# The w_v phase's pools open during the last w_k product; its data come as quarter tiles

## The chip, the cores and the metric

The kernel runs on one core of one Trainium2 chip. The metric is the device time of one execution in microseconds (us), and the median of several runs is what is compared. The engines are PE (TensorE, matrix products), DVE (VectorE), ACT (ScalarE), POOL (GpSimd) and SP (SyncE, which here only issues transfers). ACT also issues some transfers. Each engine carries out its own instructions in the order in which they stand in its queue, and an instruction that has to wait holds back all that stand behind it.

## The reference, cut to what matters

```python
# attention: batch 8, heads 8, sequence 576, head size 64
kv = einsum('bhsd,bhse->bhde', k, v); out = einsum('bhsd,bhde->bhse', q, kv)
x  = out / sqrt(mean(out**2) + 1e-6) * g_norm           # then (8, 576, 512)
# first mixture: d_model 512, d_ff 1024
k  = maximum((mu_k*x + (1-mu_k)*x_prev) @ w_k, 0)
r  = 1 / (1 + exp(-((mu_r*x + (1-mu_r)*x_prev) @ w_r)))
x  = r * ((k*k) @ w_v)
# second mixture: 4 experts, head size 64: top-2 gates, causal softmax attention in each expert
q, k, v = x @ wq[e], x @ wk[e], x @ wv[e]
out += gate[e] * (softmax(mask(q @ k.T / 8)) @ v @ wo[e])
```

The change concerns the middle part: the end of `@ w_k`, all of `@ w_v`, and the start of the second mixture.

## The kernel before

Every fp32 matrix is split into a high and a low part (`split`, L59: ACT writes the high part, L60, then DVE subtracts to get the low part, L61), and each product is three matmuls (`mm3`, L63 to L67): high·high, high·low, low·high.

The work runs through three phases. `phase_a` (L172) does attention and then, for each batch 0 to 7, the groups of w_r (`r_group`, 8 of them) and of w_k (`k_group`, 16 of them, 12 matmuls each). A `k_group` ends in ACT's `rl` (relu, L444), POOL's `ksq` (the square, L446) and a store to DRAM, `kkd`; an `r_group` ends in a store `sgd`. `phase_v` (L605) loads them back, per batch, as `kin` (two halves of the sequence, 1152 KB each, `load`, L126) and `sgv` (1152 KB, `load_s`, L132), multiplies by w_v and stores the result as `x2d`. `phase2` is the second mixture, which reads `x2d`.

The product with w_v is Strassen's scheme with seven products of quarter matrices. The left operands a11, a12, s1, s2, s4, a22, s3 were made from w_v long before and stay in SBUF. The right operands of a batch are made by `prep(b)` (L137): the quarters b11, b21, b12, b22 of `kin` and the differences t1 to t4 (`tv`, L149, on DVE for t1, t2 and on POOL for t3, t4), each split into a `kk` tile by ACT (L60) and DVE (L61). The `kk` tiles rotate through 5 buffers. `products(b)` issues seven products of 24 matmuls each (`prod`, L616 to L622), two output halves m = 0, 1 of 12 matmuls; results lie in PSUM banks `acc`, of which there are 8. Product 1 (a11·b11) stays in its bank `qa` and is added to by product 4 (s2·t2) and product 7 (s3·t3); product 3 (s1·t1) stays in `qd` and is added to by product 5 (s4·b22). ACT copies what has to be kept (`vp`, `vq`, `vu`, L626); DVE adds the parts (`ct`, L631), POOL multiplies by the gate in `sgv` (L633).

In the course of `phase_v` the weights of the second mixture are loaded too (`weights2`, L69 to L112): `wst` tiles in 2 buffers (4 of w_qk, 4 of w_vg, 2 of w_o; load L88), scaled on DVE for w_qk (L90), and split by ACT and DVE (`wqh`, `wgh`, `woh` on ACT; `wql`, `wgl`, `wol` on DVE). So are the first rows of the second mixture: `x20i` (L690) from `x2d` of batch 0, split into `x20h` on ACT (L698). A scheduler that works from a modelled timeline chooses the order on every engine; the order in the program gives only what depends on what. So `weights2`, which the program starts at batch 1, and `x20i`, which it names at batch 7, stand much earlier in the queues than in the program.

PSUM and SBUF are handed out by pools. The pool of `phase_v`, `sbv`, and its 8 banks opened after `phase_a` had closed its own; only the first batch's `kin` (pool `k0`, opened at L601 in batch 6) and three operands of it (`first_prep`, run at n = 12, 15, 18 of batch 7's groups, L588) were made earlier. `phase2` starts on ACT with loads `x2in` (L721, one buffer), their split `x2h` (L727; the low part `x2l` on POOL, L728), the copies `qs`, `ks` of the q and k products, and the exponentials `pr` (L854).

## Time and profile before

| | |
|---|---|
| median of 3 runs | 1027.13 us (1027.01 to 1028.32) |
| the profiled execution | 1032.2 us, of which the span from the first to the last instruction is 1030.3 us |
| PE busy | 974.2 us, 95% of the span |
| DVE, ACT, POOL busy | 646.0, 540.8, 417.5 us |
| mean granted clock of TensorE | 0.974 of full speed |
| w_v products on PE | 450.0 to 640.4 us of the span |

A row of a timeline gives the start, the duration, the engine, the line and the operation, and in brackets how long the engine had sat idle and what it had waited for. Matmuls overlap by their pipeline, so the count of matmuls in a stretch says more of PE than its busy time. Lines are those of the kernel before; in the kernel after they are shifted by 1 to 8.

### The profile page before, as it was taken

How to read it: one execution, taken by the hardware profiler on the slowest of the kernel's cores; microseconds unless marked ns; L12 is line 12 of the kernel's file. 1: busy time of each engine (PE TensorE's matmuls, PEld its weight loads, DVE VectorE, ACT ScalarE, POOL GpSimd, SP SyncE). 2: the span in 40 equal slices, each digit the busy share in tenths (PEclk: the TensorE clock that was granted, in tenths of full speed). 3: DMA queues.
4: the chain of work that ended last, by engine and by line, in shares of the span. 5: the costliest groups of instructions: out<-in, count | busy, mean ns of one | idle time of the engine just before them, and what ended most of it. 6: DMA issues, size and time to landing. Idle time of an engine off the chain costs nothing.

```text
span 1030.3 us, 21148 instructions
## 1 busy us (share of the span) xinstructions
PE 974.2 (95%) x7960; PEld 886.0 (86%) x7960; DVE 646.0 (63%) x1538; ACT 540.8 (52%) x1334; POOL 417.5 (41%) x510
## 2 busy tenths in 40 slices
PE   5679899999999999999899999799999999999998
PEld 3359879999999999999799999788989898888886
DVE  4868976455362638239999995366565655656552
ACT  4656755555565556444454443255553635464544
POOL 0005544131222314267777786255251615344321
PEclk9889988999999999999989999899999999999999
DMA  9463362635536225257756631200110202020102
GB/s 349 153 193 125 130 209 81 207 108 181 166 124 206 89 76 167 99 193 251 247 202 213 229 139 47 93 22 27 67 59 36 81 13 93 3 92 26 48 13 81
DMA packets 80180, 127.20 MB, mean 123 GB/s; under 512 B 7120, under 2 KB 57808, under 8 KB 78032
## 3 DMA queue, kind: packets, MB, share of 16 engines
q1 hardware_dynamic: 60592, 97.68, 28.0%
q10 hardware_dynamic: 19488, 28.19, 8.4%
q8 instruction: 63, 1.03, 0.4%
q14 instruction: 37, 0.30, 0.1%
HBM read 78.66 MB, written 47.19 MB: 122 GB/s over the span
## 4 chain that ended last, share of the span: by engine, by line
PE 67%; DMA 12%; DVE 7%; ACT 5%; POOL 5%; issue 2%; SPq 0%; ACTq 0%; DVEq 0%; POOLq 0%
PE acc L65 15%; PE acc L66 14%; PE acc L67 14%; PE acc L621 12%; DMA x2in<-x2d 3%; PE acc L918 3%; PE pt L891 3%; PE s L842 2%; DMA vraw<-in_w_v 2%; ACT pr L854 2%; POOL x2l L728 2%; POOL pr L871 2%; DMA kin<-kkd 2%; PE po L313 1%; DMA kt<-in_k 1%
## 5 line engine op out<-in xcount | busy, mean ns | idle before, releaser
L446 POOL TENSOR_TENSOR ksq<-rl 128x288 f32<-128x288 f32 x128 | 96.5, 756 | 173.8 <-ACT rl L444 141.8
L66 PE MATMUL acc<-mixl,wkh 128*128 128x288 f32 x512 | 154.3, 301 | 0.0
L65 PE MATMUL acc<-mixh,wkh 128*128 128x288 f32 x512 | 152.7, 298 | 0.0
L67 PE MATMUL acc<-mixh,wkl 128*128 128x288 f32 x512 | 151.7, 296 | 0.0
L854 ACT ACTIVATE pr<-pr,nm 128x256 f32<-128x256 f32 (+4 forms) x144 | 83.2, 580 | 75.0 <-DVE nm L808 74.0
L871 POOL TENSOR_SCALAR pr<-pr,rc,wg 128x512 f32<-128x512 f32 (+3 forms) x128 | 76.7, 615 | 104.7 <-DVE wg L801 46.2
L621 PE MATMUL acc<-kk,wh_s 128*128 128x288 f32 x512 | 104.7, 299 | 7.1 <-ACT vq L626 4.9
L409 DVE TENSOR_TENSOR mixl<-xm,mixh 128x288 fp32r<-128x288 f32 x120 | 57.2, 512 | 86.3 <-ACT mixh L417 86.3
L633 POOL TENSOR_TENSOR sgv<-ct,sgv 128x288 f32<-128x288 f32 x64 | 93.3, 1483 | 36.5 <-DVE ct L631 34.9
L66 PEld LDWEIGHTS acc<-mixl,wkh 128*128 128x128 f32 x512 | 97.2, 190 | 1.6
L444 ACT ACTIVATE rl<-acc 128x288 f32<-128x288 f32 x128 | 51.7, 406 | 87.8 <-PE acc L67 80.3
L67 PEld LDWEIGHTS acc<-mixh,wkl 128*128 128x128 f32 x512 | 97.6, 191 | 0.0
L65 PEld LDWEIGHTS acc<-mixh,wkh 128*128 128x128 f32 x512 | 97.1, 190 | 0.1
L621 PEld LDWEIGHTS acc<-kk,wh_s 128*128 128x128 f32 x512 | 83.1, 190 | 8.2 <-ACT vq L626 5.5
L65 PE MATMUL acc<-mixh,wrh 128*128 128x288 f32 x256 | 79.5, 311 | 0.5 <-ACT rl L444 0.5
L621 PE MATMUL acc<-kk,wh_a 128*128 128x288 f32 x384 | 78.5, 299 | 0.0
L808 DVE CUSTOM_DVE_ANT_0 pr<-s,mask 128x256 f32<-128x256 f32 (+4 forms) x144 | 66.9, 481 | 17.0 <-PE pt L891 13.2
L67 PE MATMUL acc<-mixh,wrl 128*128 128x288 f32 x256 | 76.8, 300 | 0.0
L66 PE MATMUL acc<-mixl,wrh 128*128 128x288 f32 x256 | 76.5, 299 | 0.2 <-ACT mixl L407 0.2
L621 PE MATMUL acc<-kk,wl_s 128*128 128x288 f32 x256 | 76.0, 297 | 0.0
L65 PE MATMUL acc<-x2h,wqh 128*128 128x320 f32 (+1 forms) x240 | 74.4, 310 | 0.0
L66 PE MATMUL acc<-x2l,wqh 128*128 128x320 f32 (+1 forms) x240 | 71.0, 296 | 0.0
(201 smaller groups left out, 2687.4 us busy)
## 6 DMA issues: line engine op xcount, KB each, us to landing
kkd<-ksq SPq DMA_DIRECT2D x128, 144.0 KB, 1.7
kin<-kkd SPq DMA_DIRECT2D x16, 1152.0 KB, 6.3
qt<-in_qT SPq DMA_DIRECT2D x32, 288.0 KB, 4.7
sgd<-sg ACTq DMA_DIRECT2D x64, 144.0 KB, 3.0
sgv<-sgd SPq DMA_DIRECT2D x8, 1152.0 KB, 5.2
x2d<-sgv SPq DMA_DIRECT2D x8, 1152.0 KB, 4.6
out<-ob SPq DMA_DIRECT2D x28, 288.0 KB, 2.1
kt<-in_k SPq DMA_DIRECT2D x24, 256.0 KB, 4.9
```

What stands on the lines that cost most here:

```text
L65: nc.tensor.matmul(ps, wh(i), xh(i), start=(i == 0), stop=False)
L66: nc.tensor.matmul(ps, wh(i), xl(i), start=False, stop=False)
L67: nc.tensor.matmul(ps, wl(i), xh(i), start=False, stop=(i == n - 1))
L409: nc.vector.tensor_sub(xl[:, p, :], xp, xh[:, p, :].bitcast(F32))
L444: nc.scalar.activation(rl, acc[:, :HS], AF.Relu)
L446: nc.gpsimd.tensor_mul(sq, rl, rl)
L621: nc.tensor.matmul(q[:, :HS], a[:, i, ms_], c[:, i, :], start=(start and i == 0 and n == 0), stop=(stop and i == KH - 1 and n == 2), skip_ ...
L633: nc.gpsimd.tensor_mul(g, c, g)
L808: nc.vector.tensor_tensor_reduce(out=pr[:R, k0:k0 + kn], in0=s[:R, :kn], in1=mk, scale=1.0, scalar=lo, op0=ALU.add, op1=ALU.min, accum_out ...
L854: nc.scalar.activation(pr[:, :L], pr[:, :L], AF.Exp, bias=nm, scale=-1.0, accum_out=sms[b, p, j][:, e2:e2 + 1])
L871: nc.gpsimd.tensor_scalar(pr[:, :L], pr[:, :L], rc[:, r:r + 1], wg, op0=ALU.mult, op1=ALU.mult)
L891: nc.tensor.transpose(pt[:, (i - i0) * P:(i - i0 + 1) * P], pr[:, k1 - P:k1], ident)
```

## The change

- The pool of `phase_v` (`sbv`) and its PSUM pool (`psv`) open in the middle of batch 7, at its first `k_group` (n = 8), after the pools of the attention front and of w_r (`psf`, `fr`, `w1`) have been closed. To make that possible the pools change sides in SBUF (`vb`, `fr`, `w1`, `sbv` right; `wk`, `w2`, `x2p` left) and the tiles `mix`, `rl`, `ksq` move to the `wk` pool.
- PSUM is split. Four banks `acc` of `phase_a` are kept through `phase_v`. The four banks of the front (`po`) become two banks `qa` and two banks `qd`, which serve only products 1, 4, 7 and products 3, 5. Before, all of these took turns in 8 banks.
- `load(0)` is issued there, and `first_prep` is `prep(0)`, run one step behind each `k_group` from n = 13 on, so that all seven operands of batch 0 are in the program before the last `k_group`.
- `kin` comes as four quarter tiles of 576 KB (5 buffers) in place of two halves (3 buffers), `sgv` as two halves of 576 KB (3 buffers) in place of one tile (2 buffers). `x2d` is stored in two halves, the first after product 5, the second at the end of the batch.
- `weights2` starts at batch 2 in the program, not at batch 1.

```diff
@@ load, load_s
-                kin[b, h] = pools[-1].tile([P, KF, HS], F32, name="kin", bufs=3 if b else 2)
-                nc.sync.dma_start(kin[b, h], kkd[b][:, :, h * HS:(h + 1) * HS])
+                for i in range(2):
+                    kin[b, i, h] = W["sv"].tile([P, KH, HS], F32, name="kin", bufs=5)
+                    nc.sync.dma_start(kin[b, i, h], kkd[b][:, KH * i:KH * i + KH, h * HS:(h + 1) * HS])
-            sgt[b] = pools[-1].tile([P, KD, S], F32, name="sgv", bufs=2)
-            nc.sync.dma_start(sgt[b], sgd[b])
+            for i in range(2):
+                sgt[b, i] = W["sv"].tile([P, KD // 2, S], F32, name="sgv", bufs=3)
+                nc.sync.dma_start(sgt[b, i], sgd[b][:, 2 * i:2 * i + 2, :])
@@ prep
-            hl = pools[-1].tile([P, 2, KH, HS], F32R, name="kk", bufs=5 if len(pools) > 1 else 3)
+            hl = W["sv"].tile([P, 2, KH, HS], F32R, name="kk", bufs=5)
@@ phase_a
-                    po = ps.tile([P, 2, 512], F32, name="po", bufs=2)
+                    po = pf.tile([P, 2, 512], F32, name="po", bufs=2)
+                first_prep = iter(())
                 for n, (g, h, m) in enumerate(groups):
+                    if not nxt and n == 2 * KD:
+                        for _ in mk:
+                            pass
+                        stf.close()
+                        W["st"] = ExitStack()
+                        W["sv"] = W["st"].enter_context(tc.tile_pool(name="sbv", bufs=1, side="right", reuse_waits="tile"))
+                        W["psv"] = W["st"].enter_context(tc.tile_pool(name="psv", bufs=1, space=PSUM, reuse_waits="tile"))
+                        load(0)
+                        first_prep = prep(0)
                     g(b, h, m)
-                    if not nxt and n in (12, 15, 18):
+                    if n > 2 * KD + 3:
                         run(first_prep)
@@ phase_v
-                def bank():
-                    return ps.tile([P, 512], F32, name="acc", bufs=8)
+                def bank(name="acc"):
+                    if name == "acc":
+                        return W["acc"].tile([P, 512], F32, name="acc", bufs=4)
+                    return W["psv"].tile([P, 512], F32, name=name, bufs=2)
-                    qa[m] = bank()
+                    qa[m] = bank("qa")
-                    qd[m] = bank()
+                    qd[m] = bank("qd")
+                nc.sync.dma_start(x2d[b][:, :2, :], sgt[b, 0])
...
-                nc.sync.dma_start(x2d[b], sg)
+                nc.sync.dma_start(x2d[b][:, 2:, :], sgt[b, 1])
-                if b == 1:
-                    W["k0"].close()
+                if b == 2:
                     w2 = weights2()
-                    if b > 0 and n in (1, 3, 5):
+                    if b > 1 and n in (1, 3, 5):
                         run(w2)
```

What the scheduler makes of it on the engines: up to the last groups of batch 7 the orders are the same. Then three places differ that matter here.

PE, at the end of `phase_a`. Before, the last of batch 7's `k_group`s (`mixh`, `mixl` by `wkh`, `wkl`) is followed by product 1 of batch 0:

```order
L65 MATMUL acc<-mixh,wkh 128x288
L66 MATMUL acc<-mixl,wkh 128x288
L67 MATMUL acc<-mixh,wkl 128x288
L621 MATMUL acc<-kk,wh_a_93 128x288 x2
L621 MATMUL acc<-kk,wl_a_94 128x288
L621 MATMUL acc<-kk,wh_a_93 128x288 x2
```

After, four of the 16 `k_group`s are left when product 1 begins; here is the one between the two parts of it and the change to product 3 (`qd`):

```order
L65 MATMUL acc<-mixh,wkh 128x288
L66 MATMUL acc<-mixl,wkh 128x288
L67 MATMUL acc<-mixh,wkl 128x288
L629 MATMUL qa<-kk,wh_a_93 128x288 x2
L629 MATMUL qa<-kk,wl_a_94 128x288
L629 MATMUL qa<-kk,wh_a_93 128x288 x2
L629 MATMUL qa<-kk,wl_a_94 128x288
L629 MATMUL qa<-kk,wh_a_93 128x288 x2
L629 MATMUL qa<-kk,wl_a_94 128x288
L629 MATMUL qd<-kk,wh_s_97 128x288 x2
L629 MATMUL qd<-kk,wl_s_98 128x288
```

So 30 matmuls of w_v have moved ahead of the last 36 of w_k, and from batch 1 on product 2, whose banks are `acc`, now begins before product 1, whose banks are `qa`: per batch 20 matmuls of product 2, 12 of product 1 (m = 0), 4 of product 2, 8 of product 3 (`qd`), then 12 of product 1 (m = 1).

ACT, where it splits the weights of the second mixture between the copies and operands of w_v. Before, in batches 1 and 2 (`vp`, `vq`, `vu` are the kept copies; `kk` the operands):

```order
L60 ACTIVATE wqh<-wst 128x512
L626 ACTIVATE vu<-acc 128x288
L60 ACTIVATE wqh<-wst 128x512
L60 ACTIVATE kk<-kin 128x1152
L626 ACTIVATE vu<-acc 128x288
L60 ACTIVATE wgh<-wst 128x260
L60 ACTIVATE kk<-tv 128x1152 x2
L60 ACTIVATE wgh<-wst 128x260
L626 ACTIVATE vu<-acc 128x288
L698 ACTIVATE x20h<-x20i 128x256 x4
L60 ACTIVATE kk<-kin 128x1152
L626 ACTIVATE vu<-acc 128x288
```

After, in batch 1, `vq` to the last `vu`:

```order
L634 ACTIVATE vq<-qd 128x288
L60 ACTIVATE kk<-kin 128x1152
L634 ACTIVATE vq<-qd 128x288
L60 ACTIVATE wgh<-wst 128x260
L634 ACTIVATE vu<-qa 128x288
L60 ACTIVATE woh<-wst 128x512
L60 ACTIVATE kk<-kin 128x1152
L634 ACTIVATE vu<-qa 128x288
L703 ACTIVATE x20h<-x20i 128x256 x4
L60 ACTIVATE kk<-tv 128x1152 x2
L60 ACTIVATE woh<-wst 128x512
L634 ACTIVATE vu<-qa 128x288
```

The first `wqh` has moved from behind batch 0's last `vu` to behind its first `vu`, and the last `woh` from behind batch 2's second `vq` to ahead of batch 1's last `vu`. The order of the kinds among themselves is the old one: `wqh`, `wgh`, then `woh` and `x20h` between operands.

ACT, at the start of the second mixture, before:

```order
L727 ACTIVATE x2h_8054<-x_7806 128x320 x4
L60 ACTIVATE qs<-acc 128x256
L60 ACTIVATE ks<-acc 128x256
L721 DMA x2in<-x2d_58 128x4x256
L727 ACTIVATE x2h_8296<-x2in 128x256 x4
L721 DMA x2in<-x2d_58 128x4x320
L854 ACT_TABLE_LOAD
L854 ACTIVATE pr,sm<-pr,nm 128x128 x2
L854 ACTIVATE pr,sm<-pr,nm 128x256 x2
L60 ACTIVATE qs<-acc 128x320
L60 ACTIVATE ks<-acc 128x320
```

and after:

```order
L734 ACTIVATE x2h_8110<-x_7860 128x320 x4
L60 ACTIVATE qs<-acc 128x256
L60 ACTIVATE ks<-acc 128x256
L728 DMA x2in<-x2d_58 128x4x256
L734 ACTIVATE x2h_8352<-x2in 128x256 x4
L728 DMA x2in<-x2d_58 128x4x320
L60 ACTIVATE qs<-acc 128x320
L861 ACT_TABLE_LOAD
L861 ACTIVATE pr,sm<-pr,nm 128x128 x2
L861 ACTIVATE pr,sm<-pr,nm 128x256 x2
L60 ACTIVATE ks<-acc 128x320
```

The copy `qs` of 320 columns has moved ahead of the table load and of the four exponentials; `ks` has stayed behind them.

On SP, the loads of batch 1's `kin` and the first half of its `sgv` stand among the last `kkd` stores, where they stood behind them; the `wst` loads stand behind the last `kkd` store in both. The load of `x20i` stands behind the first `wst` of w_o, and before it stood behind the second `wst` of w_vg.

## Rows read from the trace of the kernel before

**Rows 1.** The page, part 1: busy us (share of the span) xinstructions of each engine.
```profile
PE 974.2 (95%) x7960; PEld 886.0 (86%) x7960; DVE 646.0 (63%) x1538; ACT 540.8 (52%) x1334; POOL 417.5 (41%) x510
```

**Rows 2.** Windows of 10 us: per engine busy (xinstructions), then PEclk, DMA share, GB/s.
```profile
480.00:490.00 10.00, 10.00 (x77) 10.00 (x76) 10.00 (x11) 2.93 (x4) 7.74 (x6) 1.00 0.95 333
490.00:500.00 10.00, 9.48 (x71) 9.24 (x70) 9.72 (x12) 5.45 (x8) 3.46 (x4) 1.00 0.59 211
500.00:510.00 10.00, 8.30 (x63) 8.07 (x62) 8.46 (x8) 5.37 (x12) 10.00 (x7) 1.00 0.73 231
510.00:520.00 10.00, 5.10 (x25) 4.52 (x25) 9.68 (x10) 5.93 (x10) 8.46 (x6) 0.67 0.80 287
520.00:530.00 10.00, 10.00 (x65) 10.00 (x64) 8.69 (x8) 4.20 (x5) 5.38 (x4) 0.82 0.34 121
```

**Rows 3.** Waits in 485 to 530: who waited for what, us, times, longest.
```profile
PE acc L621 <- ACT vq L626: 4.9, 2, 3.1
PE acc L621 <- DVE ct L631: 1.7, 1, 1.7
ACT wgh L60 <- DMA wst<-in_w_vg: 7.9, 3, 3.3
ACT wqh L60 <- DVE wst L90: 7.2, 2, 6.7
ACT woh L60 <- DMA wst<-in_w_o: 3.4, 1, 3.4
```

**Rows 4.** Timeline of ACT: start, us, line, operation [idle before <-releaser].
```profile
510.33 0.42 ACT L60 ACTIVATE wgh<-wst 128x260 fp32r<-128x260 f32 x1 [3.33 <-DMA wst<-in_w_vg]
```

**Rows 5.** Timeline of DVE around the first products.
```profile
450.18 1.36 DVE L149 TENSOR_TENSOR tv<-kin,tv 128x1152 f32<-128x1152 f32 x1 [28.46 <-PE acc L67]
458.29 3.47 DVE L61 TENSOR_TENSOR kk<-tv,kk 128x1152 fp32r<-128x1152 f32 x1
474.81 2.86 DVE L90 TENSOR_SCALAR wst<-wst 128x256 f32<-128x256 f32 x2
```

**Rows 6.** DMA issues in 445 to 512: xcount, KB each, us from issue to landing.
```profile
kin<-kkd SPq DMA_DIRECT2D x7, 1152.0 KB, 6.2
wst<-in_w_qk SPq DMA_DIRECT2D x4, 256.0 KB, 6.7
x20i<-x2d SPq DMA_DIRECT2D x1, 512.0 KB, 7.1
```

**Rows 7.** Windows: one steady batch of w_v products.
```profile
579.80:602.10 22.30, 22.30 (x170) 22.30 (x169) 20.86 (x18) 11.02 (x15) 18.02 (x11) 1.00 0.63 213
```

**Rows 8.** Timeline of DVE in the steady loop.
```profile
575.40 3.38 DVE L61 TENSOR_TENSOR kk<-kin,kk 128x1152 fp32r<-128x1152 f32 x1
578.71 0.45 DVE L631 TENSOR_TENSOR ct<-acc,vq 128x288 f32<-128x288 f32 x1
601.20 0.45 DVE L631 TENSOR_TENSOR ct<-acc,vq 128x288 f32<-128x288 f32 x1
```

**Rows 9.** Timeline of PE where product 1 of a steady batch begins.
```profile
573.14 0.43 PE L621 MATMUL acc<-kk,wh_a 128*128 128x288 f32 x2
```

**Rows 10.** Timeline of ACT at the start of the last phase.
```profile
655.41 1.28 ACT L854 ACT_TABLE_LOAD   x1 [2.55 <-POOL x2l L728]
658.47 0.41 ACT L60 ACTIVATE qs<-acc 128x320 fp32r<-128x320 f32 x1
```

**Rows 11.** Timeline of PE at the same place.
```profile
659.46 0.58 PE L65 MATMUL acc<-wgh,x2h 128*128 128x260 f32 x1 [5.71 <-DVE qs L61]
```

**Rows 12.** Windows: TensorE right behind that.
```profile
657.00:663.00 6.00, 3.54 (x16) 3.54 (x17) 1.94 (x7) 2.21 (x10) 0.58 (x2) 0.50 0.27 99
```

**Rows 13.** DMA issues in 640 to 645.
```profile
x2d<-sgv SPq DMA_DIRECT2D x1, 1152.0 KB, 5.2
x2in<-x2d ACTq DMA_DIRECT2D x1, 512.0 KB, 8.0
```

**Rows 14.** DMA issues in 655 to 760, the 512 KB loads.
```profile
x2in<-x2d ACTq DMA_DIRECT2D x2, 512.0 KB, 4.0
```

More of the change, by code (lines that the diff above doesn't have):

```diff
@@ L122, in tile_kernel @@
     blk = {}
-    kin, ops, sgt, pools = {}, {}, {}, []
+    kin, ops, sgt = {}, {}, {}
     def load(b):
@@ L147, in diff @@
         def diff(x, y, eng):
-            t = pools[-1].tile([P, KH, HS], F32, name="tv", bufs=2 if len(pools) > 1 else 1)
+            t = W["sv"].tile([P, KH, HS], F32, name="tv", bufs=2)
             eng.tensor_sub(t, x, y)
             return t
-        operand("b11", quarter(0, 0))
+        b11, b21, b12, b22 = [kin[b, i, h] for h in range(2) for i in range(2)]
+        operand("b11", b11)
         yield
-        operand("b21", quarter(1, 0))
-        t1 = diff(quarter(0, 1), quarter(0, 0), nc.vector)
+        operand("b21", b21)
+        t1 = diff(b12, b11, nc.vector)
         yield
@@ L157, in prep @@
         yield
-        t2 = diff(quarter(1, 1), t1, nc.vector)
+        t2 = diff(b22, t1, nc.vector)
         operand("t2", t2)
-        t4 = diff(t2, quarter(1, 0), nc.gpsimd)
+        t4 = diff(t2, b21, nc.gpsimd)
         yield
-        operand("b22", quarter(1, 1))
-        t3 = diff(quarter(1, 1), quarter(0, 1), nc.gpsimd)
+        operand("b22", b22)
+        t3 = diff(b22, b12, nc.gpsimd)
         yield
@@ L355, in scaled @@
                     for a in range(2):
-                        po = ps.tile([P, 2, 512], F32, name="po", bufs=2)
+                        po = pf.tile([P, 2, 512], F32, name="po", bufs=2)
                         for i in range(2):
@@ L399, in mix @@
                 xT = xTs[b]
-                xh, xl = mixed[b, h, which] = [sb.tile([P, KD, HS], F32R, name=f"mix{u}", bufs=3) for u in "hl"]
+                xh, xl = mixed[b, h, which] = [wk.tile([P, KD, HS], F32R, name=f"mix{u}", bufs=3) for u in "hl"]
                 def low(p):
@@ L667, in products @@
                     gated(1, m, 0, sub, u3, qc[m][:, :HS])
-                nc.sync.dma_start(x2d[b], sg)
+                nc.sync.dma_start(x2d[b][:, 2:, :], sgt[b, 1])
                 yield
-            pools.append(sb)
+            load_s(0)
             load(1)
-            load_s(0)
-            for _ in first_prep:
-                pass
             for b in range(B):
@@ L701, in phase_v @@
                     pass
+        W["st"].close()
+        W["ps"].close()
         W["vb"].close()
```

44 lines of the change are left out of this document (19 added, 25 removed).

## The prediction

> **What bounds the kernel now.** I read the page's busy times first: PE is busy 95% of the span [rows 1], so apart from places where PE stands still nothing but fewer matmuls could help, and the change takes none away. So the question is where PE stands still, or runs at half clock, near the code that is touched. The windows show one such place inside the w_v products [rows 2]: PE starts 77 matmuls in 480–490, as in any full window, then 71, 63, 25 and 65. That is (6 + 14 + 52 + 12) = 84 short. A batch of w_v is 7 × 24 = 168 matmuls, and the same `ct` stands at 578.71 and again at 601.20 one batch later [rows 8], so a matmul takes 22.49 / 168 = 0.134 us; 84 of them are **11.2 us lost**. The granted clock shows that idle time is only part of it: 0.67 and 0.82 of full speed in 510–530 [rows 2]; the waits give 4.9 + 1.7 = 6.6 us of idle PE [rows 3], so 4.6 us are half clock and small waits. Who is late? PE waits for ACT's copy `vq` (4.9 us) [rows 3]. It is late because ACT stands at the head of its queue before the split of a weight tile, `wgh` or `woh`, whose load has not landed: 7.9 and 3.4 us in that stretch, and 7.2 us for a tile that DVE has not scaled [rows 3]; one of these rows is [rows 4]. So it is the second mixture's weights, not the w_v data, that hold PE.
>
> The second place is the start of the last phase: PE idle 5.71 us until 659.46 [rows 11], then 16 matmuls in 657 to 663 at clock 0.50 [rows 12].
>
> The third reading is what the change's first sentence aims at: at 450, when the w_v products begin, DVE has sat idle for 28.46 us [rows 5]. This is time in which first operands could be made. PE itself does not stop there.
>
> **The change part by part.**
>
> *Early pools and first operands.* Batch 7's 16 `k_group`s are 192 matmuls, 25.7 us, up to 450.0. With the pools open at the first of them, the loads of `kin` go out at about 424.3; the quarters other than b11 lie where the weights of w_r lay and are free when the last `r_group` has ended, at the same time. 6.2 us of landing [rows 6] bring b11 to about 431, its two halves of the split to 432 or 433, long before the 13th `k_group` (443.6) that product 1 now follows. I expect no wait of PE. But the matmuls are the same: 30 of w_v go ahead of 36 of w_k, and the sum is unchanged. What can be gained is a lead of the operands over PE, and there are five `kk` buffers for seven operands; the first is free only when PE is through with its product. In before DVE is at the t3 operand of batch 0 at 458.29 [rows 5]; in after the buffer that t3 needs (b11's) is free at about 455 to 458, when PE has ended product 1 and ACT has come by. So DVE stands at about the same point at 460 in both: **the early start by itself is worth 0** (bounds −1 and +3). Its use is that batch 1's loads leave the queue before 455.
>
> *Weights of the second mixture.* The last `kkd` store goes out at about 452 and the first two `wst` behind it, in both. In before the first scale stands at 474.81 [rows 5], behind DVE's work on two batches' operands. With 6.7 us to land [rows 6] and DVE free at about 461.8 (458.29 + 3.47, [rows 5]) it can be at about 461 to 462: the chain of ten weight tiles through two buffers begins 13 us earlier. But ACT's splits of them have moved ahead as well: the first `wqh` from behind batch 0's last `vu` to behind its first, the last `woh` from behind batch 2's second `vq` to ahead of batch 1's last `vu`; each is some 9.5 to 11 us of PE's time. So against the operands that they hold up the tiles are only 2 to 3.5 us better off. I take 2.7 us off the 6.6 of idle PE and put 0.5 on: 4.4 us left, about where batch 2 begins, since `x20h` also waits there: `x20i` now goes out behind a `wst` of w_o which waits for its buffer, at about 486, lands 7.1 us later [rows 6] at 493, and ACT's next operands, t1 of batch 2 among them, stand behind it. With less idle at one time I take 1.5 us of half clock in place of the 4.6. Bounds: 0 (the earlier chain clears it) and 11.2 (the chain is as late as before, at other places).
>
> *Banks.* In before a new accumulator took the next of 8 banks. Now product 1's m = 1 half of a batch needs the bank that DVE's `ct`, which adds `vq`, has read last in the batch before. PE has 20 + 12 + 4 + 8 = 44 matmuls ahead of it, 5.9 us. In before that `ct` stands behind a `kk` of 3.38 us and ends at 578.71 + 0.45 = 579.16 [rows 8], 6.0 us after the end of product 7, where the next product 1 begins (573.14, [rows 9]). With the start of PE behind the read that is about 0.2 us per batch, 1.3 us over six or seven batches. DVE is busy 20.86 of 22.30 us there [rows 7], so there is slack but not much. Bounds: 0, and one DVE row more per batch (below).
>
> *Sum for the w_v products:* lost 4.4 + 1.5 + 1.3 = 7.2 where 11.2 were: **4.0 us gained**, bounds 11 and −1.
>
> *Halves and quarters.* Only the last store of `x2d` is on the path to the end: the first `x2in`, 512 KB, takes 8.0 us beside the 1152 KB store [rows 13], and 4.0 us later, alone [rows 14]. So the store costs it 4.0 us, and half a store some 2.0: `x2in` lands 2 us earlier (bounds 0 and 4). The Trainium skill speaks against smaller pieces: its page DMA: Bandwidth & Descriptors (section Anatomy of one DMA, on the GpSimd path) gives each transfer a fixed 2.0 us beside its bytes at 436 GB/s. By that, as an estimate, 1152 KB would take 4.7 us and half of it 3.35, so `x2in` would land only 1.35 us earlier and the forecast would be 0.6 us higher. The rows have 5.2 us for the full store and none for a half, so they don't decide it. Quarter loads inside the loop I cost at nothing: the transfers are busy 0.63 of the time there [rows 7], and PE did not wait for one in that batch (22.30 of 22.30 us busy). Without that cover each late quarter would cost up to its landing, 6 us.
>
> *Order at the last phase's start.* `qs` now stands where the table load stands, 655.41 in place of 658.47 [rows 10]: 3.06 us. But the two banks that follow are freed by `qs` and by `ks`, and `ks` has stayed behind the exponentials. With `x2in` 2 us earlier: `qs` at 653.4, PE's next 12 matmuls at about 654.4 to 655.8; the table load and the four exponentials (3.06 us) then end at 656.8, `ks` and its low part at 657.7, and PE waits for it some 2 us. Idle 0.6 + 1.9 = 2.5 in place of 5.71, so 3.2, and perhaps 1 of the 2 us that the half clock cost (16 matmuls took 3.54 us there, [rows 12]). Against it, other orders inside the last phase changed slightly, for which nothing stands in the profile. **3.0 us**, bounds 0.5 and 5.
>
> *Together:* 4.0 + 3.0 = 7.0 us. The profiled execution took 1032.2 us, 5 above the median of the runs, with a span of 1030.3; the differences carry over to either. 1027.1 − 7.0 = **1020 us** (span of a profiled run about 1023).
>
> **The rivals.**
>
> *The stall goes altogether (1012).* If the weights' chain, 13 us earlier and with no `kin` and `sgv` in the queues beside it, lands each tile before ACT comes to it, the 11.2 us go, 1.3 stay for the banks: 9.9 + 4 to 5 at the last phase's start. For it: each ACT wait for a tile's load is 3.4 us at most [rows 3]. Against: the splits moved too, and two buffers serve ten tiles.
>
> *The stall only moves (1024).* ACT waits for `wst` and `x20i` as long as before, in batch 1 in place of batch 2: 0 to 0.5 gained there, 3 at the last phase's start. For it: the kinds stand in the same order on ACT, and the buffers are two as before.
>
> *Nothing in sum (1027).* The stall only moves, and `ks` behind the exponentials takes back what `qs` gives, or the first products wait 2 to 3 us for a quarter of `kin` (the change would then not do what it says: first operands not there early).
>
> *Slower (1030).* The fixed banks bind PE to DVE. In the loop the `ct` that frees product 1's bank comes 0.2 us late by my reckoning. If one more 128x1152 instruction of DVE falls ahead of it, or the `kk` of 3.38 us [rows 8] is as long twice, it is 1.6 us or more per batch; six batches are 10 us: 1020 + 10 = 1030. It decides from the point where that `ct` ends more than 5.9 us after product 7, and DVE's work per batch passes 22.4 (20.86 now). For it: only 1.4 us of slack per batch, and DVE also splits the weights' low parts in two of the batches. Against: DVE's order in the loop is the same as before.
>
> **How the numbers follow.** 0.2% is 2.05 us, about what a measurement of this kernel can tell from no change: 1025.1 to 1029.2. My forecast (1016 to 1022.5) 0.47; stall gone (below 1016) 0.14; stall only moves (1022.5 to 1025) 0.13; nothing in sum (1025.1 to 1029.2) 0.13; slower 0.13. So faster 0.47 + 0.14 + 0.13 = 0.74, same 0.13, slower 0.13. The range from 1013 to 1029 leaves out a little of the first rival and most of the last.
>
> **What would show it.** The windows of the w_v products: PE's shortage below 84 matmuls, some 50 by my sum, and no row at clock 0.5 longer than 3 us. The first `wst` scale on DVE at 460 to 463. ACT's waits for `wst` and `x20i` still there, 3 to 6 us in sum, about where batch 2 begins. PE idle before product 1's second half each batch: 0 to 0.3 us. `x2in` landing in 6 us or so beside the half store, PE idle for `ks` about 2 us. No idle PE in 440–455. I am wrong if the stretch 485–530 is as thin as before (the stall moved), if it is full (the stall gone), or if every batch shows an idle PE until `ct` (the banks).

## The result, and the profile of the kernel after

The change makes the kernel faster: **1015.36 us** median (1013.47 to 1018.54) beside 1027.07 us (1026.87 to 1028.32), a ratio of 0.9887 [0.986, 0.9913], or 11.7 us. The forecast was 1020 us, in a range of 1013 to 1029: the sign and the range held, and the gain is 4.7 us larger than the 7.0 forecast. It lies just below the band of 1016 to 1022.5 us to which the forecast gave its largest chance. The profiled execution of the kernel after took 1015.07 us (span 1013.2), close to its median; that of before ran 5 us above its own. So the two profiles differ by 17.1 us of span, more than the kernels do.

The page, part 1, of the kernel after, to read beside [rows 1] (busy us, share of the span, x instructions):

```profile
PE 966.5 (95%) x7960; PEld 877.9 (87%) x7960; DVE 638.1 (63%) x1538; ACT 540.6 (53%) x1334; POOL 417.1 (41%) x510
```

The matmuls are the same 7960, and the share of PE is the same 95%. The gain lies in two places, the w_v products and the start of the last phase, as the forecast had it.

**The w_v products.** Windows of 10 us of the kernel after, to read beside [rows 2] (columns: PE, PEld, DVE, ACT, POOL busy with x instructions, PEclk, DMA share, GB/s):

```profile
470.00:480.00 10.00, 8.48 (x63) 8.14 (x62) 10.00 (x11) 5.70 (x10) 8.47 (x5) 1.00 0.77 223
480.00:490.00 10.00, 10.00 (x77) 10.00 (x76) 10.00 (x12) 4.92 (x10) 2.81 (x3) 1.00 0.87 288
490.00:500.00 10.00, 9.45 (x71) 9.17 (x69) 8.10 (x8) 5.74 (x10) 9.41 (x7) 1.00 0.44 166
500.00:510.00 10.00, 8.29 (x62) 8.09 (x61) 8.98 (x7) 5.21 (x9) 10.00 (x7) 1.00 0.77 235
510.00:520.00 10.00, 10.00 (x78) 10.00 (x77) 10.00 (x10) 5.17 (x7) 7.07 (x5) 1.00 0.60 199
```

Where [rows 2] had 84 matmuls too few, these windows have 14 + 6 + 15 = 35, against 77 for a full one, and no window is below the full clock (1.00 is 2.4 GHz); before it was 0.67 and 0.82. PE's idle rows there are three, 3.8 us in sum (timeline of PE: start, us, line, operation, in brackets the idle time before it and what ended it):

```profile
477.13 0.53 PE L629 MATMUL qa<-kk,wh_a 128*128 128x288 f32 x2 [1.52 <-DVE ct L639]
497.40 0.54 PE L629 MATMUL qa<-kk,wh_a 128*128 128x288 f32 x2 [0.56 <-DVE ct L639]
501.91 0.54 PE L629 MATMUL qa<-kk,wh_a 128*128 128x288 f32 x2 [1.72 <-DVE ct L639]
```

All three wait for the `ct` of DVE that reads the bank `qa`. In [rows 3] the larger part, 4.9 of 6.6 us, was for ACT's `vq`. The waits in 455 to 510 (who waited for what: us, times, longest), with ACT's beside [rows 3]:

```profile
ACT wgh L60 <- DMA wst<-in_w_vg: 4.9, 3, 2.4
ACT wqh L60 <- DVE wst L90: 4.5, 2, 2.9
PE qa L629 <- DVE ct L639: 3.8, 3, 1.7
ACT x20h L703 <- DMA x20i<-x2d: 2.7, 1, 2.7
ACT woh L60 <- DMA wst<-in_w_o: 0.8, 1, 0.8
```

ACT still waits 4.9 + 4.5 + 0.8 = 10.2 us for weights (18.5 before, [rows 3]) and 2.7 for `x20i`. None of these rows is named as what PE waits for. What makes the `ct` late is not told by them; DVE itself is busy 10.00 of 10.00 us in three of the five windows.

**The start of the last phase.** The timeline of ACT in the kernel after, to read beside [rows 10]:

```profile
644.03 0.44 ACT L60 ACTIVATE qs<-acc 128x320 fp32r<-128x320 f32 x1 [2.64 <-PE s L849]
644.49 1.28 ACT L861 ACT_TABLE_LOAD   x1
647.56 0.41 ACT L60 ACTIVATE ks<-acc 128x320 fp32r<-128x320 f32 x1
```

The timeline of PE, beside [rows 11]:

```profile
648.55 0.40 PE L65 MATMUL acc<-wgh,x2h 128*128 128x260 f32 x1 [1.39 <-DVE ks L61]
```

The DMA issues in 630 to 640 (x count, KB each, us from issue to landing), beside [rows 13]:

```profile
x2d<-sgv SPq DMA_DIRECT2D x1, 576.0 KB, 3.4
x2in<-x2d ACTq DMA_DIRECT2D x1, 512.0 KB, 5.1
```

And a window of six microseconds there, beside [rows 12]:

```profile
647.00:653.00 6.00, 4.61 (x37) 3.90 (x36) 3.71 (x17) 1.83 (x9) 0.00 (x0) 1.00 0.03 12
```

`qs` stands ahead of the table load, `x2in` lands in 5.1 us in place of 8.0, PE is idle 1.39 us for `ks` in place of 5.71 for `qs`, and it starts 37 matmuls at full clock in the six microseconds where [rows 12] had 16 at half clock.

**Two stretches.** For every kernel below three stretches of the profiled execution are given. A is from the span's start to the first `r_group` matmul of batch 7: code that no kernel here changes. B is from there to the end of the last w_v matmul: 1632 matmuls, of which each takes 22.40 / 168 = 0.1333 us in a steady batch of before, so 217.6 us if PE never stops. C is the rest. "Idle" is PE's idle rows in B, in sum; a row has a bracket only from 0.15 us on.

| kernel | median us | A | B | idle in B | C | PE idle where C's first `x2h` products begin |
|---|---|---|---|---|---|---|
| before | 1027.07 | 411.7 | 228.8 | 7.1 | 389.8 | 5.71, `qs` |
| after | 1015.36 | 408.3 | 223.7 | 3.8 | 381.2 | 1.39, `ks` |

A differs by 3.4 us though the code is the same; over all kernels below it goes from 406.7 to 411.9. So about 5 us of a span are scatter of one execution, and B and C are what can be compared: B gained 5.1, C 8.6. Together that is 2 us more than the medians show, the uncertainty with which the two shares are known. They scatter too: `a_fat` (below) has in B the same order of instructions on every engine as after, and its B is 225.1 beside 223.7. So a difference of 1.4 us in B, between two single profiles, is not to be read.

### The profile page after: what moved, and what is told of

Its sections match the earlier page's. It is cut to its first block, busy times and chain, and to the rows that moved or that the text cites. A ratio compares the mean times of both kernels' runs of the same rounds, so it can differ in the third digit from the quotient of the medians.

```text
span 1013.2 us, 21245 instructions
## 1 busy us (share of the span) xinstructions
PE 966.5 (95%) x7960; PEld 877.9 (87%) x7960; DVE 638.1 (63%) x1538; ACT 540.6 (53%) x1334; POOL 417.1 (41%) x510
## 4 chain that ended last, share of the span: by engine, by line
PE 73%; DVE 8%; DMA 8%; ACT 5%; POOL 4%; issue 2%; SPq 0%; ACTq 0%; DVEq 0%; POOLq 0%
PE acc L65 15%; PE acc L66 15%; PE acc L67 14%; PE qa L629 6%; PE qd L629 4%; PE acc L629 4%; PE pt L898 3%; PE acc L925 3%; DMA x2in<-x2d 3%; PE s L849 3%; POOL x2l L735 2%; ACT pr L861 2%; DMA vraw<-in_w_v 2%; PE po L314 1%; POOL pr L878 1%
## 5 line engine op out<-in xcount | busy, mean ns | idle before, releaser
L641 POOL TENSOR_TENSOR sgv<-ct,sgv 128x288 f32<-128x288 f32 x64 | 82.4, 1313 | 35.2 <-DVE ct L639 34.7
L67 PE MATMUL acc<-x2h,wql 128*128 128x320 f32 (+1 forms) x240 | 71.1, 296 | 0.0
L61 DVE TENSOR_TENSOR kk<-tv,kk 128x1152 fp32r<-128x1152 f32 x32 | 59.0, 1861 | 8.8 <-ACT kk L60 8.8
L898 PE MATMUL pt<-ident,pr 128*128 128x128 f32 x400 | 62.7, 276 | 1.1 <-ACT pt L907 0.5
L418 ACT ACTIVATE mixh<-xm 128x288 fp32r<-128x288 f32 x128 | 52.3, 443 | 10.2 <-DVE xm L417 10.1
```

The costliest lines, as they stand in the source:

```text
L61: nc.vector.tensor_sub(lo, src, hi.bitcast(F32))
L67: nc.tensor.matmul(ps, wl(i), xh(i), start=False, stop=(i == n - 1))
L641: nc.gpsimd.tensor_mul(g, c, g)
L898: nc.tensor.transpose(pt[:, (i - i0) * P:(i - i0 + 1) * P], pr[:, k1 - P:k1], ident)
```

## The experiments

Medians of before were 1026.66 to 1027.49 us beside them; ratios are to before, with a 95% interval. No kernel leaves work out; `a_fat` adds a store.

| kernel | median us | ratio | A | B | idle in B | C |
|---|---|---|---|---|---|---|
| b_banks | 1026.72 | 0.9992 [0.9978, 1.0005] | 411.7 | 227.0 | 5.3 | 388.5 |
| a_u3 | 1017.15 | 0.9905 [0.9887, 0.9924] | 411.9 | 223.9 | 4.7 | 382.9 |
| a_coarse | 1038.86 | 1.0112 [1.0094, 1.013] | 408.4 | 239.6 | 14.6 | 389.6 |
| b_half | 1018.03 | 0.9914 [0.9898, 0.993] | 407.0 | 222.0 | 3.0 | 387.1 |
| b_pieces | 1021.58 | 0.9953 [0.9935, 0.9972] | 406.7 | 225.7 | 4.2 | 387.1 |
| a_kinhalf | 1031.46 | 1.0048 [1.0032, 1.0063] | 407.3 | 237.2 | 12.3 | 381.4 |
| a_fat | 1023.49 | 0.9975 [0.9962, 0.9987] | 410.3 | 225.1 | 5.1 | 389.8 |
| a_wst6 | 1018.69 | 0.9931 [0.9911, 0.9951] | 409.1 | 224.0 | 2.5 | 386.2 |
| a_scale | 1018.18 | 0.9904 [0.9889, 0.9919] | 410.1 | 224.2 | 2.6 | 382.8 |
| bh_scale | 1016.50 | 0.9895 [0.9882, 0.9908] | 408.6 | 220.8 | 2.0 | 385.9 |
| bh_q | 1014.31 | 0.9879 [0.9861, 0.9898] | 408.0 | 221.2 | 2.6 | 382.5 |
| a_q | 1019.75 | 0.9935 [0.9913, 0.9957] | 408.5 | 223.9 | 3.9 | 384.9 |

### The banks alone (b_banks)

On the kernel before: `qa` and `qd` get two fixed banks each, four stay for the rest.

```diff
-def bank(): return ps.tile([P, 512], F32, name="acc", bufs=8)
+def bank(name="acc"): return ps.tile([P, 512], F32, name=name, bufs=4 if name == "acc" else 2)
-    qa[m] = bank()
+    qa[m] = bank("qa")        # and qd[m] = bank("qd")
```

> The kernel before with one part of the change alone: products 1, 4, 7 in two banks qa, products 3, 5 in two banks qd, four banks acc for the rest; pools, loads and stores as before. Theory A (the fixed banks cost time: in the trace of after all three idle rows of PE in 470 to 505 wait for the DVE subtraction that reads qa last): PE idles for that subtraction here too, on top of the waits for the weights, 1029 to 1033. Theory B (the banks cost nothing, PE would wait for the same DVE work at another place): 1026.5 to 1028.

Measured: no change in the time (theory B), though the wait that theory A named came. The idle moves; the waits of PE in 470 to 535 are no longer for `vq`:

```profile
PE qa L621 <- DVE ct L631: 5.1, 3, 3.1
```

And the steady batch becomes longer on PE. The window of one batch of the kernel after, which has these banks:

```profile
552.27:574.98 22.71, 22.71 (x171) 22.43 (x169) 19.39 (x18) 10.91 (x16) 18.04 (x11) 1.00 0.64 208
```

And of `bh_q` (below), whose banks rotate as in before:

```profile
568.24:590.64 22.40, 22.40 (x170) 22.40 (x169) 19.39 (x18) 10.35 (x15) 19.39 (x11) 1.00 0.63 211
```

From PE's starts the steady batch is 22.40 us in before, `b_half`, `b_pieces`, `bh_scale` and `bh_q`, and 22.70 to 22.75 in `b_banks`, in after and in the kernels made from it with the same pieces and banks (all but `a_u3`, `a_kinhalf` and `a_coarse`): the fixed banks cost **0.32 us a batch** where they act. No idle row shows it. It lies in two matmul rows that are longer than their neighbours (0.43), here in the timeline of PE of the kernel after:

```profile
569.54 0.53 PE L629 MATMUL qa<-kk,wh_a 128*128 128x288 f32 x2
574.98 0.65 PE L629 MATMUL acc<-kk,wh_a 128*128 128x288 f32 x2
```

The two rows of DVE's timeline that these wait for:

```profile
569.05 0.44 DVE L639 TENSOR_TENSOR ct<-qa,vq 128x288 f32<-128x288 f32 x1
573.60 1.58 DVE L61 TENSOR_TENSOR kk<-tv,kk 128x1152 fp32r<-128x1152 f32 x1
```

The first, +0.10, begins when the `ct` that frees its bank is through (569.05 + 0.44 = 569.49). The second, +0.22, goes on when the low part of its operand is there (573.60 + 1.58 = 575.18): with fixed banks a `ct` stands ahead of that split on DVE (573.23, that is behind it in `bh_q`).

### A bank freed by ACT instead of DVE (a_u3)

On the kernel after: DVE's last `ct` reads the copy `u3`, so that `qa` is free when ACT has copied it.

```diff
-gated(1, m, 1, add, qa[m][:, :HS], p5[m])
+gated(1, m, 1, add, u3, p5[m])
```

> The kernel after, but the last addition of a batch reads the copy vu, which ACT makes of the bank qa anyway, in place of the bank itself; so the bank is free for the next batch's product 1 when ACT has copied it, and not when DVE has come to its addition. Theory A (fixed banks tie PE to DVE): the three idle rows of 0.6 to 1.7 us behind batches 0 and 1 go, 1011 to 1013. Theory B (PE is short of operands from DVE in any case, the bank is only where it shows): the idle time moves to another wait, 1014.5 to 1016.

Measured: B as without the edit (223.9 beside 223.7), and a median above both ranges. The waits for `ct` are gone and others stand in their place (waits in 465 to 520):

```profile
PE qd L629 <- ACT vq L634: 4.0, 2, 2.6
```

So the bank that DVE holds is where PE's wait is recorded; it isn't what makes the work late. Its batches behind 525 take 22.40 us again, up to the last two, so what the bank cost there is given back; about as much is lost ahead of them. A new cost came with it: DVE reads two operands in SBUF, and that instruction takes 2.92 us where the same sum with one operand in a bank takes 0.44 (569.05, above). DVE was busy 22.44 of a batch's 22.78 us. The row of DVE's timeline:

```profile
571.90 2.92 DVE L639 TENSOR_TENSOR ct<-vu,vq 128x288 f32<-128x288 f32 x1
```

### Large pieces in the early pools (a_coarse, a_kinhalf)

On the kernel after. `a_coarse` takes every piece back to its old size: `kin` in halves through two buffers (three halves don't fit beside what the pool holds), `sgv` whole, one `x2d` store. `a_kinhalf` does it for `kin` alone.

```diff
-kin[b, i, h] = W["sv"].tile([P, KH, HS], F32, name="kin", bufs=5)
-nc.sync.dma_start(kin[b, i, h], kkd[b][:, KH * i:KH * i + KH, h * HS:(h + 1) * HS])
+t = W["sv"].tile([P, KF, HS], F32, name="kin", bufs=2)
+nc.sync.dma_start(t, kkd[b][:, :, h * HS:(h + 1) * HS])
```

> The kernel after with whole pieces again: kin as two halves of 1152 KB (2 buffers, since 3 don't fit), sgv as one tile of 1152 KB (2 buffers), x2d stored once at the end of the batch; early pools and banks as in after. Theory A (the gain inside the w_v products comes from pools that open early, so that batch 1's loads and the first weights leave the queue early, not from the size of the pieces): the w_v products take as long as in after within 2 us, and only the last phase's start gives back 2 to 3 us: 1017 to 1019. Theory B (small pieces are what lets the loads pass each other): the stretch behind the first batch is as thin as in the kernel before, 1022 to 1026.

> The kernel after with kin as two halves of 1152 KB in 2 buffers (3 don't fit beside the pools that are still open); sgv, x2d, pools and banks as in after. The kernel after with whole pieces throughout took 1038.9 and PE idled 1.1 to 1.8 us in every batch for the subtraction that reads qa, while DVE waited for kin. Theory G (the quarter tiles are what makes the early pools bearable: without them DVE waits for kin and PE, tied to DVE by the fixed banks, for DVE): that idle time in every batch again, 234 us or more from batch 7's w_r groups to the end of the w_v products, 1026 to 1031 in all. Theory H (it was the whole sgv and x2d that held the loads up): 1015 to 1018.

Measured: both are slower than the kernel before, by 11.9 us (outside both ranges) and 4.8 us (theory G, just above its range), and B is 13 to 16 us longer than in after. The executions of `a_kinhalf` go from 1027.78 to 1035.12 us, and the profiled one is the fastest. The waits in 505 to 630 of `a_kinhalf`:

```profile
DVE tv L149 <- DMA kin<-kkd: 11.8, 5, 3.9
ACT kk L60 <- DMA kin<-kkd: 8.4, 4, 2.5
PE qa L630 <- DVE ct L640: 6.8, 8, 1.9
```

And its longest idle row of PE, near the start of the stretch:

```profile
477.01 0.85 PE L630 MATMUL qa<-kk,wh_a 128*128 128x288 f32 x2 [4.98 <-DVE ct L640]
```

The loads come late, DVE and ACT wait for them, and PE then waits for the `ct` behind them in almost every batch. From one product 1 to the next, behind 528, PE's batches are 23.7 to 24.2 us in `a_kinhalf`, 24.5 to 25.1 in `a_coarse`, against 22.40. So within the early pools, with the room that they leave, the quarter tiles are needed. What two buffers cost and what the size costs is not told apart here.

### Only the half stores (b_half), and all the pieces (b_pieces), without the early pools

On the kernel before. `b_half` stores `x2d` in two halves, the first after product 5, and changes nothing else:

```diff
     gated(0, m, 1, add, qd[m][:, :HS], u2[m])
+nc.sync.dma_start(x2d[b][:, :2, :], sg[:, :2, :])
 ...
-nc.sync.dma_start(x2d[b], sg)
+nc.sync.dma_start(x2d[b][:, 2:, :], sg[:, 2:, :])
```

`b_pieces` has `kin` in quarters (5 buffers) and `sgv` in halves (3 buffers) as well.

> The kernel before with x2d stored in two halves, the first after product 5; everything else as before, so on ACT the copy qs still stands behind the table load and the exponentials at the start of the last phase. Theory C (the half store makes the last phase start earlier): x2in lands 2 to 3 us earlier, PE's idle time of 5.7 us falls to 3 or so, 1023 to 1025. Theory D (it is the place of qs in ACT's queue): the idle time stays within 1 us, 1026 to 1027.5.

> The kernel before with the small pieces alone: kin as quarter tiles (4 buffers for batch 0, 5 for the others), sgv as two halves (3 buffers), x2d stored in two halves; pools, banks and the first operands as before. From the start of batch 7's w_r groups to the end of the w_v products the profiles show 228.8 us for before, 223.7 for after, 222.0 for before with the half stores alone. Theory E (early pools and fixed banks bring nothing inside the w_v products, the pieces bring it all): 221 to 224 us there, and 1017 to 1019.5 in all, since the copy qs still stands behind the exponentials at the start of the last phase. Theory F (the early pools bring several us there, and what the half stores did alone is another effect): 226 to 229 us there with the quarter loads, 1022 to 1026.

Measured: one extra store brings 9 of the 11.7 us, far more than either theory allowed. 2.7 of them are in C. The larger part is in B, 228.8 to 222.0, where PE's matmuls stand in the same order as in before. The waits of ACT there, in 480 to 525 of `b_half`:

```profile
ACT wqh L60 <- DVE wst L90: 7.1, 1, 7.1
ACT wgh L60 <- DMA wst<-in_w_vg: 4.6, 2, 3.8
ACT woh L60 <- DMA wst<-in_w_o: 3.9, 1, 3.9
PE acc L621 <- ACT vq L626: 1.3, 1, 1.3
PE acc L621 <- DVE ct L631: 1.0, 2, 0.8
```

ACT waits 7.1 + 4.6 + 3.9 = 15.6 us for weights, not much less than the 18.5 of [rows 3]; PE is idle 3.0 in place of 7.1. The other 2.7 of the 6.8 us in B are mostly the clock: it is 1.00 in every window of `b_half` from 480 to 520, where [rows 2] had 0.67 and 0.82 in 510 to 530. What differs in the rows is what stands behind a wait in ACT's queue. In the timeline of ACT in before:

```profile
515.46 0.63 ACT L60 ACTIVATE woh<-wst 128x512 fp32r<-128x512 f32 x1 [3.37 <-DMA wst<-in_w_o]
516.00 1.15 ACT L60 ACTIVATE kk<-kin 128x1152 fp32r<-128x1152 f32 x1
517.05 0.39 ACT L626 ACTIVATE vq<-acc 128x288 f32<-128x288 f32 x1
```

PE in before, at that place:

```profile
517.50 0.85 PE L621 MATMUL acc<-kk,wh_s 128*128 128x288 f32 x2 [3.13 <-ACT vq L626]
```

ACT in `b_half`, the same split with a longer wait:

```profile
506.54 0.40 ACT L626 ACTIVATE vq<-acc 128x288 f32<-128x288 f32 x1
510.85 0.63 ACT L60 ACTIVATE woh<-wst 128x512 fp32r<-128x512 f32 x1 [3.91 <-DMA wst<-in_w_o]
511.38 0.39 ACT L626 ACTIVATE vu<-acc 128x288 f32<-128x288 f32 x1
```

In before the second `vq` stood behind the wait of 3.37 us, and PE was idle 3.13 us for it. In `b_half` both `vq` are through before the wait of 3.91 us begins, and no idle row of PE answers to it. So the gain in B is not what a store costs: the scheduler put the splits elsewhere. That this place is the cause is read from these rows. SP, DVE and POOL have another order in `b_half` too, and no run changes ACT's order alone.

`b_pieces` keeps 5.1 us of gain, between the two theories: B is 225.7, with idle rows of 2.01 and 2.24 us for `ct`. Why the quarters make B worse here was not settled. C is that of `b_half`, but not for the same reason: `x2in` was issued 6.0 us after the last w_v product, when the last half store had landed, in place of 2.9, and PE was idle 5.02 us in place of 2.96; in the six microseconds behind it the clock was 0.74, in `b_half` 0.52.

### The last store and the order of the last phase (a_fat, a_q)

On the kernel after. `a_fat` adds a store of 576 KB behind the last one, into a buffer that is no longer used; `a_q` splits the last half store into two quarters:

```diff
 nc.sync.dma_start(x2d[b][:, 2:, :], sgt[b, 1])
+if b == B - 1: nc.sync.dma_start(sgd[b][:, 2:, :], sgt[b, 1])          # a_fat
-nc.sync.dma_start(x2d[b][:, 2:, :], sgt[b, 1])
+    nc.sync.dma_start(x2d[b][:, 2 + m, :], sgt[b, 1][:, m, :])         # a_q, in the loop over m
```

> The kernel after with one more store of 576 KB behind the last half store of x2d (the second half of sgv into a DRAM buffer that nothing reads any more), so that the transfers beside the first x2in are as much as with a whole store. The order at the start of the last phase is with it that of the kernel before: qs behind the table load and the exponentials. From the end of the w_v products to the end of the span the profiles show 389.8 us for before, 387.1 for before with half stores, 381.2 for after. Theory C2 (half store and place of qs together make the difference): 388 to 390 us there, 1021 to 1024 in all. Theory C3 (it is something else in after, earlier data or other banks): 381 to 384 us, 1015 to 1018.

> The kernel after with the last half store of x2d of each batch in two quarters of 288 KB. Here this turns the scheduler's choice the other way round: qs stands behind the table load and the exponentials, as in the kernel before, while pools, banks and small pieces are those of after and the last store is even smaller. Theory O (the order): 385 to 387.5 us from the end of the w_v products to the end of the span in place of 381.2, 1019 to 1022 in all. Theory P (early pools, banks): 380 to 383 us there, 1014 to 1016.5.

Measured: `a_fat` loses 8.1 us against after, and C is at 389.8, the value of before. Two things came back: `x2in` took 8.1 us beside 1152 KB of stores, and the table load stood ahead of `qs` again. Its DMA issues in 636 to 640:

```profile
x2d<-sgv SPq DMA_DIRECT2D x1, 576.0 KB, 3.3
sgd<-sgv SPq DMA_DIRECT2D x1, 576.0 KB, 7.5
x2in<-x2d ACTq DMA_DIRECT2D x1, 512.0 KB, 8.1
```

So `a_fat` (theory C2) doesn't tell them apart. `a_q` goes further: `x2in` landed in 4.3 us, even earlier than in after, but the order of the two instructions flipped, and C is 384.9, 3.7 more than in after. The timeline of ACT in `a_q`:

```profile
643.55 1.28 ACT L861 ACT_TABLE_LOAD   x1 [2.62 <-POOL x2l L735]
646.61 0.41 ACT L60 ACTIVATE qs<-acc 128x320 fp32r<-128x320 f32 x1
```

And of PE:

```profile
646.31 0.64 PE L65 MATMUL acc<-x2h,wqh 128*128 128x320 f32 x1 [2.81 <-DVE vs L778]
```

PE is idle 2.81 us, but not for `qs`: it waits for `vs`, a copy out of a bank that DVE makes at 645.83 behind a wait of 4.43 us for the first exponentials (L871). PE's own order in the last phase is not that of before either. So `a_q` (about as theory O had it) shows that the table load and the exponentials, done early, hold PE up, and not what the place of `qs` is worth by itself.

### Earlier weights (a_wst6, a_scale)

On the kernel after. `a_wst6` gives the weight tiles six buffers in place of two; `a_scale` takes the scaling of w_qk from DVE to ACT:

```diff
-st = w2.tile([P, DM], F32, name="wst", bufs=2)
+st = w2.tile([P, DM], F32, name="wst", bufs=6)                                           # a_wst6
-nc.vector.tensor_scalar(st[:, :scaled], st[:, :scaled], -D ** -0.5, None, op0=ALU.mult)
+nc.scalar.activation(st[:, :scaled], st[:, :scaled], AF.Copy, scale=-D ** -0.5)          # a_scale
```

> The kernel after with six buffers in place of two for the tiles through which the weights of the second mixture come, so that a load need not wait for the split of the tile two before it. Theory A2 (what is left of the stall behind batches 0 and 1, 3.8 us of idle PE, is still ACT held at the head of its queue by these loads): ACT's waits for them fall from 8 us or so to under 3, 1011 to 1013.5. Theory B2 (DVE's own work, 14 us of scaling and splitting in one and a half batches, is what is late): ACT's waits fall but PE idles as before for the subtraction, 1014.5 to 1016.5.

> The kernel after, with the scaling of the q and k weights (L90, four tiles) done by ACT in place of DVE. It takes 4 to 5 us of work off DVE in the stretch where PE still idles for DVE's subtractions (1.5 + 0.6 + 1.7 us in the profile of after), and ACT's wait for a scaled tile goes; ACT gets four operations of 0.4 us. Theory A3 (DVE's own work for the weights is what is late behind batches 0 and 1): the idle rows shrink to under 1.5 us in sum, from batch 7's w_r groups to the end of the w_v products 221 to 222 us in place of 223.7, 1012 to 1014 in all. Theory B3 (the order on ACT and the waits for transfers decide, DVE's total doesn't): 223 to 226 there, 1014.5 to 1018.

Measured: neither shortens B (224.0 and 224.2), and both medians lie above both ranges. In `a_wst6` the waits for the weights are almost gone, and PE waits all the same (waits in 455 to 512):

```profile
PE qa L629 <- DVE ct L639: 2.2, 1, 2.2
ACT wgh L60 <- DMA wst<-in_w_vg: 1.0, 1, 1.0
```

So in the kernel after the weights' chain isn't what PE waits for any more; what makes its `ct` late stays open. `a_wst6` has `qs` ahead of the table load as after has, but issued `x2in` 6.1 us after the last w_v product in place of 2.9, and lost 5 us in C.

### The half stores with the scale on ACT, and the other order (bh_scale, bh_q)

On `b_half`, that is, with the pools, the tile sizes and the banks of before. `bh_scale` moves the scale to ACT as above; `bh_q` also stores the last half in quarters, which flips the order at the last phase's start, this time the other way.

```diff
+    nc.sync.dma_start(x2d[b][:, 2 + m, :], sg[:, 2 + m, :])      # bh_q, in the loop over m
-nc.sync.dma_start(x2d[b][:, 2:, :], sg[:, 2:, :])
```

> The kernel before with x2d in two half stores (which took 1018.0) and the scaling of the q and k weights on ACT in place of DVE. Theory A3 (DVE's work for the weights): the three idle rows of 0.8, 1.3 and 0.8 us go, 219 to 220.5 us from batch 7's w_r groups to the end of the w_v products in place of 222.0, 1014.5 to 1016.5 in all. Theory B3 (order on ACT and transfers): 221 to 225 there, 1017 to 1021. In both the last phase keeps its 387 us, since qs still stands behind the exponentials.

> The kernel before (its own pools, banks, whole kin and sgv) with the scaling of the q and k weights on ACT, and x2d stored in three pieces: a half after product 5 and two quarters of 288 KB at the end. With quarters at the end the scheduler puts qs of 320 columns ahead of the table load and the exponentials, as in the kernel after; with a half at the end (1016.5) it didn't. Theory O (the order at the start of the last phase is worth 5 to 6 us, whatever the pools are): 380 to 382 us from the end of the w_v products to the end of the span in place of 385.9, 1010 to 1012.5 in all. Theory P (the 381 to 383 us of the kernels with early pools come from these pools or the banks): 385 to 387 us there, 1015 to 1017.5.

Measured: B is 220.8 and 221.2, the lowest of all, but within the scatter of `b_half`'s 222.0: what the scale is worth is not shown. The last phase of `bh_q`, timeline of ACT:

```profile
642.06 0.44 ACT L60 ACTIVATE qs<-acc 128x320 fp32r<-128x320 f32 x1 [2.58 <-POOL x2l L729]
642.52 1.28 ACT L855 ACT_TABLE_LOAD   x1
645.58 0.41 ACT L60 ACTIVATE ks<-acc 128x320 fp32r<-128x320 f32 x1
```

And of PE:

```profile
646.58 0.39 PE L65 MATMUL acc<-wgh,x2h 128*128 128x260 f32 x1 [1.78 <-DVE ks L61]
```

With `qs` first C is 382.5, with the table load first (`bh_scale`) 385.9: 3.4 us, about as between after and `a_q` in the other direction. It is not the smaller last store that brings it, for `x2in` landed later here (5.8 us, 5.1 in `bh_scale`); PE's order in the last phase is that of after. C and the median lie between the two theories. `bh_q` takes 1014.31 us: as fast as the kernel after within both intervals, without the early pools, the quarter tiles and the fixed banks.

## Why the prediction was right, and where its sizes were off

**The place and the lost time.** That the w_v products lose 11.2 us is confirmed by the sum over the whole stretch: 228.8 − 217.6 = 11.2. In after it is 223.7 − 217.6 = 6.1, where the forecast had 7.2: 5.1 us gained for 4.0. By its three terms: idle PE 3.8 (expected 4.4); half clock 0 in the windows shown (expected 1.5); banks 0.32 us in each of the last four batches, 1.3 in sum (expected 1.3). Of the 0.32 the wait that was reckoned, for the `ct`, is 0.10; the 0.22 for a `kk` was not foreseen, so that this sum came out is luck. The rest, some 1.0 us, is in small waits.

**The weights' chain.** It begins where it was expected, 460 to 463, or a little before:

```profile
457.95 0.38 DVE L90 TENSOR_SCALAR wst<-wst 128x256 f32<-128x256 f32 x1
```

`x20i` went out at 484.23 (expected 486), and ACT waited 2.7 us for it. ACT's waits for weights and `x20i` are 12.9 us in sum in 455 to 510; about where batch 2 begins, in 484 to 495, they are 5.9, of the 3 to 6 expected there. But the reason given for the gain, tiles that are 2 to 3.5 us earlier against the operands that they hold up, is not shown, and it isn't needed: `b_half`, whose first scale stands as far behind its first w_v product as in before, gains 6.8 us in B; `a_wst6` frees the chain and gains none. What counts in the rows of `b_half` is which copies stand behind a wait on ACT, and it is the scheduler that moved them. No run has the kernel after with a late chain. So the place and about the size of this gain were right, and the reason is at most part of it.

**Early pools worth 0.** No run has the early pools alone, so this stays open. They are not needed for the gain: `bh_scale` and `bh_q`, without them, have B at 220.8 and 221.2, `b_half` 222.0, the kernels with them and quarter tiles 223.7 to 225.1. But beside quarter tiles they may help: `b_pieces`, without the pools and the fixed banks, has 225.7, after 223.7, although the banks cost it 1.3. No PE row between 440 and 455 is idle, as expected. What the later start of the next weights does, no run shows.

**The start of the last phase: the mis-sized term.** Expected 3.0 us (bounds 0.5 and 5); C differs by 8.6 us in the profiles, outside these bounds. Its first part is the place that was reckoned. Counted in the timelines of PE to the 187th matmul of C, at which before and after have done the same products, the kernels with the whole store, or as many bytes (before, `b_banks`, `a_coarse`, `a_fat`), take 31.9 to 33.9 us, `b_half` and `bh_scale`, with the half store and the old order, 31.0 and 30.2, `a_q` 29.5, and after 27.8: 5.6 less than the 33.4 of before. There every step of the reckoning was too small. `x2in` landed in 5.1 us, not in 6; `qs` cost no idle time, where 0.6 us was put; `ks` cost 1.39, where 1.9 was put. And the half clock, of which 1 of 2 us was to be saved, went altogether: in [rows 12] 16 matmuls took 3.54 us, 0.22 each, in after 35 took the 4.45 us from 648.55 to 653, 0.13 each, at full clock. When `x2in` goes out counts as well: `a_wst6`, in the order of after, and `b_pieces`, in the old one, issued it some 3 us later and take 32.0 and 32.1 us to that point.

The second part was taken for a loss. The steps gave 3.2 + 1 = 4.2 us, and the forecast went down to 3.0 for "other orders inside the last phase". But the next 278 matmuls, to the 465th, take 35.1 us in each of the six kernels with PE's order of after (after, `a_u3`, `a_kinhalf`, `a_scale`, `bh_q`, `a_wst6`), and 36.5 in each of the other eight: that order gains 1.4 us, and it is part of the 3.4 us between `bh_scale` and `bh_q`. From there to the end the fourteen kernels take 318.3 to 320.1 us, without a pattern, so the last 1.6 of the 8.6 us are scatter.

The estimate from the Trainium skill, page DMA: Bandwidth & Descriptors, section Anatomy of one DMA, was 3.35 us for the half store and 4.7 for the whole one. The rows have 3.4 and 5.2, and 2.8 for the four half stores in 440 to 512 of after, so the trace agrees within some 0.6 us, though these stores go out on SP and the page's sum is for the GpSimd path. The load gained 2.9 us, not the 1.35 that followed from it. It took 4.0 us alone, 5.1 beside 576 KB of stores, 8.0 and 8.1 beside 1152 KB (6.8 in `b_banks`); the page's sum is for one transfer and has nothing of the bytes that move beside it.

**The rivals.** *The stall goes altogether* and *only moves*: neither; half of it went. The time does lie in the band of the first (below 1016), but it was the last phase that brought it there. *Nothing in sum*: no wait for a first quarter of `kin` was seen. *Slower*: its place was rightly named, its cause was another. In `a_coarse` and `a_kinhalf` the `ct` that frees product 1's bank comes late in nearly every batch, at 1.3 to 2.7 us a batch (1.6 was put), and the time is above that of before; but there DVE waits for the loads of `kin`, where the rival had one more instruction of DVE ahead. In the kernel after, with the quarter tiles, that `ct` is late by 0.10 us a batch.

So the forecast was right on the two places and on the sign. Its total came out 4.7 us small mostly because the last phase did; in the w_v products the sum was nearer than its reasons.

## What to carry to other kernels

A wait at the head of an in-order queue costs what stands behind it, not what it lasts: look first at which copy the bottleneck engine needs next and whether it stands ahead of or behind a load's wait. Where a scheduler sets the order, try each part of a change alone: here one extra half store brought 9 of 11.7 us, mostly by another order on the engines, and the part that the change is named after was not needed for a kernel as fast. An order that flips far from the edit is part of its effect: count it by stretches in which the same work is done. Before giving accumulators fixed banks, see how far the last reader's end is from the next write: a small overlap showed here in no idle row, only in the length of a batch.
